# Crossbar DMA transposes, a head started in halves, and matmuls moved up, in a fused attention and feed-forward kernel

The kernel runs on one core of one Trainium2 chip. The metric is device time in microseconds (us) of that core, median over executions; the lower the better. All executions told of here are fast, with a mean granted TensorE clock of 0.995 or more.

## The reference

Eight batches of eight heads, 576 rows of 64 columns. Attention is linear: q is normalized over the columns, k over the rows, both after an exponent, so that kv is a 64 x 64 matrix for each head. Its result, 4608 rows of 512 columns, goes through a gated feed-forward block.

```python
q_s = exp(q);  q_s = q_s / sum(q_s, axis=-1)          # (the reference also subtracts maxima and adds 1e-9)
k_s = exp(k);  k_s = k_s / sum(k_s, axis=2)
kv  = einsum('bhsd,bhse->bhde', k_s, v)
x   = einsum('bhsd,bhde->bhse', q_s, kv)              # then heads side by side: 4608 x 512
g, val = x @ w_gate, x @ w_val                        # 512 x 1536
out = (gelu(g) * val) @ w_out                         # 1536 x 512
```

## The kernel before

One batch follows another. A batch's feed-forward part has twelve steps (a gate and a value group of four matmuls each, then a gelu on ScalarE and a product on DVE) and four output groups of twelve matmuls. All eight PSUM banks are in two pools: six for feed-forward (`ps_big`), two for attention (`ps_att`). Attention of the next batch rides between steps, by a list of callbacks: `at(b, FI, i, ...)` runs after step i of batch b (steps count from 0), and `at(b, NS, i, ...)` after output group i. x needs q transposed, since the contraction runs over its columns. The kernel has two ways to do that: TensorE transposes (batches 0 to 2), and, from batch 3 on, DVE transposes of 32 x 32 blocks followed by 16 small DMAs that put the blocks in place.

```python
    def kv0_mm(hp):                           # batch 0: both heads of a pair in one 128-column matmul
        pool, tag = (ps_att, "att") if hp == 0 else (ps_big, "mm")
        st[("pskv0", hp)] = pool.tile([P, P], f32, name="pskv0", tag=tag)
        for n in range(NC):
            nc.tensor.matmul(
                st[("pskv0", hp)], ek_b[0][:, n, hp * P:(hp + 1) * P],
                v16_b[0][:, n, 2 * hp:2 * hp + 2, 0:D], start=(n == 0), stop=(n == NC - 1))
    # ... cut
    def unit_t32(b, hp):                      # batches 3 to 7: blocks on DVE ...
        # ... cut
        nc.vector.transpose(
            out=et[:, :, hp].rearrange("p c (n i) -> p n c i", i=32),
            in_=eq_b[b % 2][:, :, hp * P:(hp + 1) * P].rearrange("p n (c j) -> p n c j", j=32))

    def moves(b):                             # ... then 16 DMAs
        # ... cut
        for a in range(4):
            for c in range(4):
                nc.sync.dma_start(out=t[32 * c:32 * c + 32, a],
                                  in_=st[(b, "et")][32 * a:32 * a + 32, c])
    # ... cut: the start of batch 0
    cast_v(0, 0, 2, "dve")
    cast_v(0, 2, 4, "act")
    ksum_rec()
    cast_v(0, 4, 6, "act")
    kv0_mm(0); kv0_mm(1); kv0_norm(0); kv0_norm(1)
    cast_v(0, 6, 8, "dve")
    # ... cut: loads, weights
    unit_x(0, 0, "act", True)
    kv0_mm(2)
    unit_x(0, 1, "act", True)
    kv0_norm(2)
    unit_t(0, 1, "dve")
    # ... cut: what rides in batch 1
    at(1, FI, 9, L(unit_t, 2, 0))
    at(1, FI, 10, L(unit_t, 2, 1))
    at(1, FI, 11, L(load_batch, 3), L(exp, "k", 2, 4, 8), L(exp, "q", 3), L(exp, "k", 3), ...)
    at(1, NS, 0, L(unit_trem, 2))
    at(1, NS, 1, L(unit_kv4, 2))
    at(1, NS, 2, L(unit_x4, 2, ("dve", "dve")))
```

The softmax here doesn't subtract the row's maximum and nothing guards it: scores larger than these inputs give would overflow.

## Time and profile before

| | before |
|---|---|
| median of the first three runs | 315.99 us (315.94 to 316.39) |
| profiled run | 316.26 us, span 314.5 us, clock 1.0 |
| TensorE busy | 98% of the span |
| DVE, ScalarE, GpSimd busy | 61%, 44%, 14% |

The runs' times are 1.7 to 1.9 us longer than the spans that the profiler shows. In what follows, times of instructions count from the start of the span. "PE" is TensorE, "ACT" ScalarE, "POOL" GpSimd, and "SPq" the queue from which DMAs are issued. The prediction shows the main lines of before. This is TensorE's list of waits: what it waited for, us in total, how often, and the longest.

```profile
PE pskv L261 <- DVE v L143: 0.4, 1, 0.4
...
PE psx L365 <- DVE kv_sb L267: 0.2, 1, 0.2
```

Both lie in the first 15 us, before feed-forward starts. (The short stalls near 48.84 and 63.21 are not in this list; they are found from starts and counts.) And this is DVE's timeline at the start (start, length, line and operation, output and input):

```profile
14.38 0.73 DVE L143 CAST v<-vt 128x640 f16<-128x640 f32 x1
...
15.61 0.69 DVE L143 COPY eqt<-pst 128x1024 f16<-128x1024 f16 x1 [0.24 <-PE pst L306]
```

DVE casts v's last two heads from 14.38 to 15.11 us. Batch 2's feed-forward begins here on TensorE's timeline:

```profile
85.26 1.03 PE L411 MATMUL psg<-xt,wg_sb 128*128 128x512 f16 x4
```

### The profile page before, as it was taken

The numbers are of one execution on the slowest core, as the hardware profiler recorded it, in microseconds if no ns is written. First come the engines' busy times: TensorE is split into PE (matmuls) and PEld (weight loads), VectorE is DVE, ScalarE is ACT, GpSimd is POOL, SyncE is SP. The second block draws the span as 40 slices with busy tenths as digits, with TensorE's granted clock in tenths as the row PEclk, the third lists the DMA queues.
The fourth block names the chain that finished last, engine by engine and source line by source line (L and its number), as shares of the span: only waits on it lengthen the run. The fifth ranks groups of instructions, "written<-read, shape, count | busy, mean of one in ns | idle before, by whom it ended". The sixth has DMA issues, their size and how long they took to land.

```text
span 314.5 us, 4799 instructions
## 1 busy us (share of the span) xinstructions
PE 307.7 (98%) x1826; PEld 143.7 (46%) x1826; DVE 191.1 (61%) x324; ACT 138.5 (44%) x178; POOL 44.7 (14%) x59
## 2 busy tenths in 40 slices
PE   8899999999999999999999999999999999999995
PEld 3444454444444444444444444444444444444443
DVE  3844386597898479746984599458943434324331
ACT  3753564988433663356334643374330233013300
POOL 2657451331001200030003000300000000000000
PEclk9999999999999999999999999999999999999999
DMA  7999999950178116921492139303021200140002
GB/s 231 372 383 394 401 386 388 395 194 0 69 245 306 53 70 194 349 59 67 127 386 80 72 90 383 115 27 131 1 58 28 115 18 0 35 101 0 3 33 100
DMA packets 42343, 50.78 MB, mean 161 GB/s; under 512 B 3408, under 2 KB 38096, under 8 KB 42320
## 3 DMA queue, kind: packets, MB, share of 16 engines
q1 hardware_dynamic: 40592, 48.84, 45.0%
q10 hardware_dynamic: 1728, 1.64, 1.6%
q8 instruction: 14, 0.23, 0.3%
q14 instruction: 9, 0.07, 0.1%
HBM read 37.75 MB, written 9.44 MB: 150 GB/s over the span
## 4 chain that ended last, share of the span: by engine, by line
PE 90%; DVE 4%; DMA 2%; ACT 2%; issue 1%; ACTq 0%; DVEq 0%
PE psy L489 29%; PE psg L411 28%; PE psv L411 27%; DMA qt<-in_q_dram 2%; PE pskv L284 1%; DVE eq L200 1%; PE psl L510 1%; PE psx L383 1%; DVE rq L191 1%; DVE rq L181 1%; DVE ht L418 1%; PE psx L365 1%; ACT eq L163 1%; PE pst L306 1%; ACT L416 0%
## 5 line engine op out<-in xcount | busy, mean ns | idle before, releaser
L416 ACT ACTIVATE gl<-psg 128x512 f32<-128x512 f32 x108 | 64.0, 599 | 131.0 <-PE psg L411 124.5
L418 DVE SCALAR_TENSOR_TENSOR ht<-psv,gl 128x512 f16<-128x512 f32 x108 | 72.9, 682 | 64.6 <-PE psv L411 64.1
L411 PE MATMUL psg<-xt,wg_sb 128*128 128x512 f16 x384 | 100.5, 379 | 0.1
L411 PE MATMUL psv<-xt,wv_sb 128*128 128x512 f16 x384 | 100.5, 379 | 0.0
L489 PE MATMUL psy<-wo_sb,ht 128*128 128x512 f16 x420 | 94.0, 379 | 0.0
L411 PEld LDWEIGHTS <-wv_sb 128*128 128x128 f16 x432 | 42.3, 98 | 51.2 <-issue 0.8
L411 PEld LDWEIGHTS <-wg_sb 128*128 128x128 f16 x432 | 41.9, 98 | 49.4 <-issue 0.4
L489 PEld LDWEIGHTS <-ht 128*128 128x128 f16 x420 | 40.4, 98 | 47.9 <-issue 0.8
L538 DVE TENSOR_SCALAR yo<-psy 128x512 f32<-128x512 f32 x30 | 20.5, 685 | 29.7 <-PE psy L489 29.7
L139 POOL CAST v<-vt 128x640 f16<-128x640 f32 x26 | 18.8, 763 | 137.1 <-DMA vt<-in_v_dram 98.3
L181 DVE TENSOR_REDUCE rq<-eq 128x10 f32<-128x640 f16 x28 | 22.7, 812 | 6.1 <-ACT eq L163 5.7
L200 DVE TENSOR_TENSOR eq<-eq,rrq 128x640 f16<-128x640 f16 (+1 forms) x29 | 23.7, 817 | 0.3
L163 ACT ACTIVATE ek<-kt 128x1280 f16<-128x1280 f32 (+1 forms) x11 | 19.1, 1746 | 3.4 <-DMA kt<-in_k_dram 3.3
L163 ACT ACTIVATE eq<-qt 128x2560 f16<-128x2560 f32 (+2 forms) x10 | 18.4, 1863 | 2.3 <-DMA qt<-in_q_dram 2.2
L331 DVE STREAM_TRANSPOSE et<-eq 128x640 f16<-128x640 f16 x20 | 16.9, 845 | 0.7
L411 PE MATMUL psg<-xtr,wg_sb 128*128 128x512 f16 x48 | 12.3, 379 | 0.0
L411 PE MATMUL psv<-xtr,wv_sb 128*128 128x512 f16 x48 | 12.3, 379 | 0.0
L143 DVE CAST xt<-psx 128x512 f16<-128x512 f32 x16 | 10.2, 682 | 1.2 <-PE psx L365 1.2
L403 PE MATMUL pswarm<-warm,ident 128*128 128x512 f16 x34 | 9.5, 438 | 1.4 <-POOL ident masks.py:199 1.4
L163 ACT ACT_TABLE_LOAD x8 | 10.3, 1283 | 0.6 <-DMA qt<-in_q_dram 0.5
L141 ACT CAST xt<-psx 128x512 f16<-128x512 f32 x16 | 8.7, 588 | 3.5 <-PE psx L365 3.5
L141 ACT CAST xtr<-psxr 128x128 f16<-128x128 f32 (+1 forms) x6 | 1.7, 283 | 17.8 <-PE psxr L383 17.8
(74 smaller groups left out, 122.6 us busy)
## 6 DMA issues: line engine op xcount, KB each, us to landing
out_dram<-yo SPq DMA_DIRECT2D x14, 512.0 KB, 3.5
kt<-in_k_dram SPq DMA_DIRECT2D x7, 640.0 KB, 7.9
vt<-in_v_dram SPq DMA_DIRECT2D x7, 640.0 KB, 8.4
qt<-in_q_dram SPq DMA_DIRECT2D x7, 640.0 KB, 6.5
qt<-in_q_dram SPq DMA_DIRECT2D x8, 512.0 KB, 6.7
eqt<-et SPq DMA_DIRECT2D x80, 40.0 KB, 1.9
wost<-in_moe_w_out_dram SPq DMA_DIRECT2D x6, 512.0 KB, 7.9
kt<-in_k_dram SPq DMA_DIRECT2D x6, 512.0 KB, 8.1
```

Of the source, the lines that this page charges most:

```text
L139: nc.gpsimd.tensor_copy(out=dst, in_=src)
L141: nc.scalar.copy(out=dst, in_=src)
L143: nc.vector.tensor_copy(out=dst, in_=src)
L163: nc.scalar.activation(out=dst[:, n0:NC, h0 * D:h1 * D].rearrange(o, d=D, **({"t": 2} if b >= QUAD else {})), in_=heads(tiles[(nm, b)], b, ...
L181: nc.vector.reduce_sum(rq, e, axis=mybir.AxisListType.X)
L200: (nc.gpsimd if eng == "pool" else nc.vector).tensor_tensor(out=e, in0=e, in1=rrq.unsqueeze(-1).to_broadcast((P, n, 2, D)), op=ALU.mult)
L331: nc.vector.transpose(out=et[:, :, hp].rearrange("p c (n i) -> p n c i", i=32), in_=eq_b[b % 2][:, :, hp * P:(hp + 1) * P].rearrange("p n ...
L411: nc.tensor.matmul(ps, w[:, ci, fi * P:(fi + 1) * P], xt[:, ci, :], start=(ci == 0), stop=(ci == HP - 1))
L416: nc.scalar.activation(out=gl, in_=psg, func=ACTF.Gelu)
L418: nc.vector.scalar_tensor_tensor(out=ht, in0=psv, scalar=_H_SCALE, in1=gl, op0=ALU.mult, op1=ALU.mult)
L489: nc.tensor.matmul(psy, hts[fi][:, ns * P:(ns + 1) * P], wo_sb[:, fi, :], start=(fi == 0), stop=(fi == NFI - 1))
L538: nc.vector.tensor_scalar(out=yo, in0=psy, scalar1=1.0 / _H_SCALE, scalar2=None, op0=ALU.mult)
```

## The change

Its intent is to take work and stalls off TensorE in the first 85 us: (1) start batch 0's feed-forward earlier, (2) have batch 1's x ready when its feed-forward begins, (3) give one step of batch 1 other PSUM banks, (4) move batch 2's transposes from TensorE to one crossbar DMA, and (5) do the same for batches 3 to 7, where they ran on DVE. (6) is a consequence: batch 3's loads are queued behind batch 2's transpose, and batch 3's sums move into batch 2's first steps. The numbers are those of the prediction.

```diff
@@ (4), (5) the crossbar transpose, one DMA for a batch @@
+    def unit_td(b):
+        t = att.tile([P, NC * C], f16, name="eqt", tag="eqt").rearrange(
+            "p (n h t) -> p n h t", n=NC, h=HP)
+        nc.sync.dma_start_transpose(out=t.rearrange("p n h t -> p (n h) t"),
+                                    in_=eq_b[b % 2].rearrange("p n c -> p (n c)"))
+        st[(b, "eqt4")] = t
@@ (1) kv of batch 0 in halves @@
+            for s in range(2):
+                c0 = hp * P + s * D
+                nc.tensor.matmul(ps[s * D:(s + 1) * D], ek_b[0][:, n, c0:c0 + D],
+                                 v16_b[0][:, n, 2 * hp + s, 0:D], start=(n == 0), stop=(n == NC - 1))
@@ (1) the start (old lines: see above) @@
+    cast_v(0, 0, 1, "dve")
+    cast_v(0, 1, 2, "act")
+    cast_v(0, 2, 3, "dve")
+    cast_v(0, 3, 4, "act")
     cast_v(0, 4, 6, "act")
+    unit_t(0, 1, None, (lambda: kv0_mm(0), lambda: kv0_norm(0), lambda: kv0_mm(1),
+                        lambda: kv0_norm(1), lambda: unit_x_halves(0, 0)))
+    evac_t1 = st["evac_t"]
+    unit_x(0, 1, "act", True)
+    kv0_mm(2)
+    evac_t1("dve")
+    ksum_rec(1)
+    kv0_norm(2)
     cast_v(0, 6, 8, "dve")
@@ (2) end of batch 0, start of batch 1 @@
-    at(0, NS, 16, L(unit_kv, 1, 0), L(cast_v, 1, 4, 8), L(load_batch, 2, ((v, "v"),)))
-    at(0, NS, 6, L(norm, 1, 3))
+    at(0, NS, 16, L(unit_kv, 1, 0), L(cast_v, 1, 4, 8), L(load_batch, 2, ((v, "v"),)),
+       L(norm, 1, 3))
-                cut = 10 if ns == 3 else NFI
+                cut = 9 if ns == 2 else 7 if ns == 3 else NFI
@@ (3) @@
-            hts.append(ffn_fi(xt, fi))
+            hts.append(ffn_fi(xt, fi, b == 1 and fi == 7))     # True: both banks from ps_att
@@ (4), (6) batch 2 @@
-    at(1, FI, 3, L(exp, "q", 2), L(norm, 2, 0))                # and so for steps 4 to 6
+    at(1, FI, 3, L(exp, "q", 2), L(norm, 2, 0, "pool"))
-    at(1, FI, 9, L(unit_t, 2, 0))
-    at(1, FI, 10, L(unit_t, 2, 1))
+    at(1, FI, 9, L(unit_td, 2))
     at(1, FI, 11, L(load_batch, 3), ...)
-    at(1, NS, 0, L(unit_trem, 2))
-    at(1, NS, 1, L(unit_kv4, 2))
-    at(1, NS, 2, L(unit_x4, 2, ("dve", "dve")))
+    at(1, NS, 0, L(unit_kv4, 2))
+    at(1, NS, 1, L(unit_x4, 2, ("dve", "dve")))
@@ (5), (6) batches 3 to 7 @@
-                at(b - 1, NS, hp, L(norm_sum, n, hp))
-                at(b, FI, hp, L(norm_mul, n, hp), L(unit_t32, n, hp))
-            at(b, FI, 4, L(moves, n))
+                at(*((b, FI, hp) if n == 3 else (b - 1, NS, hp)), L(norm_sum, n, hp))
+                at(b, FI, hp, L(norm_mul, n, hp))
+            at(b, FI, 4, L(unit_td, n))
```

Cut are two smaller parts of (1) (sums of k in two tiles, x of the first head pair in two banks) and of (2) (the order of the matmuls that open batch 1), and tile sizes.

More of the change, by code (lines that the diff above doesn't have):

```diff
@@ L103 @@
     QUAD = 2
-    T32 = 3
     def heads(x, b, h0, h1):
@@ L122 @@
     wst = {}
-    ETW = HP * 4 * NC * 32
     def wst_tile(name, n, w):
-        t = wstp.tile([P, ETW], f16, name=name, tag="wst")
-        return t[:, 0:2 * n * w].bitcast(f32).rearrange("p (n w) -> p n w", n=n)
+        return wstp.tile([P, HP * 256], f32, name=name, tag="wst")[:, 0:n * w].rearrange(
+            "p (n w) -> p n w", n=n)
     def load_w_gv(c):
@@ L236, in kv_norm @@
         for j in range(2):
-            kv_sb = att.tile([P, 2, D], f16, name="kv_sb", tag="kv", bufs=12)
+            kv_sb = att.tile([P, 2, D], f16, name="kv_sb", tag="kv", bufs=8)
             nc.vector.scalar_tensor_tensor(
@@ L242, in kv_norm, with ksum_mm, ksum_rec @@
             st[(b, "kv", 2 * g + j)] = kv_sb
-    def ksum_mm(hps):
-        if "pks" not in st:
-            st["pks"] = ps_big.tile([P, HP], f32, name="pks", tag="mm")
-        for hp in hps:
+    def ksum_mm(g):
+        st[("pks", g)] = ps_big.tile([P, 2], f32, name="pks", tag="mm")
+        for j in range(2):
+            hp = 2 * g + j
             for n in range(NC):
-                nc.tensor.matmul(st["pks"][:, hp:hp + 1], ek_b[0][:, n, hp * P:(hp + 1) * P], ones,
-                                 start=(n == 0), stop=(n == NC - 1))
-    def ksum_rec():
-        st["rck0"] = att.tile([P, HP], f32, name="rck0", tag="rck0", bufs=1)
-        nc.vector.reciprocal(out=st["rck0"], in_=st["pks"])
+                nc.tensor.matmul(st[("pks", g)][:, j:j + 1], ek_b[0][:, n, hp * P:(hp + 1) * P],
+                                 ones, start=(n == 0), stop=(n == NC - 1))
+    def ksum_rec(g):
+        st[("rck0", g)] = att.tile([P, 2], f32, name="rck0", tag="rck0")
+        nc.vector.reciprocal(out=st[("rck0", g)], in_=st[("pks", g)])
     def kv0_mm(hp):
-        pool, tag = (ps_att, "att") if hp == 0 else (ps_big, "mm")
-        st[("pskv0", hp)] = pool.tile([P, P], f32, name="pskv0", tag=tag)
+        ps = ps_big.tile([P, D], f32, name="pskv0", tag="mm")
+        st[("pskv0", hp)] = ps
         for n in range(NC):
-            nc.tensor.matmul(
-                st[("pskv0", hp)], ek_b[0][:, n, hp * P:(hp + 1) * P],
-                v16_b[0][:, n, 2 * hp:2 * hp + 2, 0:D], start=(n == 0), stop=(n == NC - 1))
+            for s in range(2):
+                c0 = hp * P + s * D
+                nc.tensor.matmul(ps[s * D:(s + 1) * D], ek_b[0][:, n, c0:c0 + D],
+                                 v16_b[0][:, n, 2 * hp + s, 0:D], start=(n == 0), stop=(n == NC - 1))
     def kv0_norm(hp):
-        kv_sb = att.tile([P, 2, D], f16, name="kv_sb", tag="kv", bufs=12)
+        kv_sb = att.tile([P, 2, D], f16, name="kv_sb", tag="kv", bufs=8)
         nc.vector.scalar_tensor_tensor(
-            out=kv_sb, in0=st[("pskv0", hp)].rearrange("p (h e) -> p h e", e=D),
-            scalar=st["rck0"][:, hp:hp + 1], in1=mask, op0=ALU.mult, op1=ALU.mult)
+            out=kv_sb, in0=st[("pskv0", hp)].unsqueeze(1).to_broadcast((P, 2, D)),
+            scalar=st[("rck0", hp // 2)][:, hp % 2:hp % 2 + 1], in1=mask, op0=ALU.mult, op1=ALU.mult)
         st[(0, "kv", hp)] = kv_sb
@@ L295, in get_eqt, with unit_t @@
         if (b, "eqt") not in st:
-            st[(b, "eqt")] = att.tile([P, HP * 4 * NC * 32], f16, name="eqt", tag="eqt")[
+            st[(b, "eqt")] = att.tile([P, NC * C], f16, name="eqt", tag="eqt")[
                 :, 0:HP * S].rearrange("p (h t) -> p h t", h=HP)
         return st[(b, "eqt")]
-    def unit_t(b, g, eng="dve"):
+    def unit_t(b, g, eng="dve", between=()):
         eqt = get_eqt(b)
         pst = ps_att.tile([P, 2, MAIN], f16, name="pst", tag="att")
+        st["evac_t"] = lambda eng: copy_on(eng, eqt[:, 2 * g:2 * g + 2, 0:MAIN], pst)
         for j in range(2):
             hp = 2 * g + j
+            for f in between if j == 1 else ():
+                f()
             for n in range(NM):
@@ L308, in unit_t @@
                     eq_b[b % 2][:, n + 1, hp * P:(hp + 1) * P], ident)
-        st["evac_t"] = lambda eng: copy_on(eng, eqt[:, 2 * g:2 * g + 2, 0:MAIN], pst)
         if eng:
@@ L324, in unit_trem @@
         nc.vector.tensor_copy(out=st[(b, "eqtr")], in_=pst[:, :, 0:REM] if b == 0 else pst[:, :, 0:P:2])
-    def unit_t32(b, hp):
-        if (b, "et") not in st:
-            st[(b, "et")] = wstp.tile([P, 4, HP, NC * 32], f16, name="et", tag="wst")
-        et = st[(b, "et")]
-        nc.vector.transpose(
-            out=et[:, :, hp].rearrange("p c (n i) -> p n c i", i=32),
-            in_=eq_b[b % 2][:, :, hp * P:(hp + 1) * P].rearrange("p n (c j) -> p n c j", j=32))
-    def moves(b):
-        t = att.tile([P, HP * 4 * NC * 32], f16, name="eqt", tag="eqt").rearrange(
-            "p (a h x) -> p a h x", a=4, h=HP)
-        for a in range(4):
-            for c in range(4):
-                nc.sync.dma_start(out=t[32 * c:32 * c + 32, a],
-                                  in_=st[(b, "et")][32 * a:32 * a + 32, c])
-        t = t.rearrange("p a h (n i) -> p h n a i", i=32)
-        st[(b, "eqt5")] = t
+    def unit_td(b):
[4 more added lines that the diff above has]
+        st[(b, "eqt4")] = t
     def xq(b, hp):
-        if (b, "eqt5") in st:
-            return st[(b, "eqt5")][:, hp, 1:NC]
+        if (b, "eqt4") in st:
+            return st[(b, "eqt4")][:, 1:NC, hp]
         return st[(b, "eqt")][:, hp, 0:MAIN]
     def xqr(b, hp):
-        if (b, "eqt5") in st:
-            return st[(b, "eqt5")][:, hp, 0, :, 0:32:2]
+        if (b, "eqt4") in st:
+            return st[(b, "eqt4")][:, 0, hp, 0:P:2]
         return st[(b, "eqtr")][:, hp, :]
@@ L367, in unit_x, with unit_x_halves @@
         copy_on(eng, xt[:, hp, :], psx)
+    def unit_x_halves(b, hp):
+        for i, eng in enumerate(("act", "dve")):
+            c = slice(i * MAIN // 2, (i + 1) * MAIN // 2)
+            psx = ps_big.tile([P, MAIN // 2], f32, name="psx", tag="mm")
+            nc.tensor.matmul(psx, st[(b, "kv", hp)].rearrange("p h e -> p (h e)"),
+                             xq(b, hp)[:, c], start=True, stop=True)
+            copy_on(eng, get_xt(b)[:, hp, c], psx)
     def unit_xrem(b, eng="act"):
@@ L420, in gate, with ffn_fi, ffn_first @@
         return ht
-    def ffn_fi(xt, fi):
-        psg = ps_big.tile([P, 512], f32, name="psg", tag="mm")
+    def ffn_fi(xt, fi, spare=False):
+        pool, tag = (ps_att, "att") if spare else (ps_big, "mm")
+        psg = pool.tile([P, 512], f32, name="psg", tag=tag)
         mm_gv(psg, wg_sb, xt, fi, range(HP))
-        psv = ps_big.tile([P, 512], f32, name="psv", tag="mm")
+        psv = pool.tile([P, 512], f32, name="psv", tag=tag)
         mm_gv(psv, wv_sb, xt, fi, range(HP))
         return gate(psg, psv)
-    def ffn_first(xt, after, between):
+    def ffn_first(xt, after):
         ps = []
@@ L440, in ffn_first @@
                 mm_gv(psg, wg_sb, xt, fi, range(0, 2))
-                for f in between[fi]:
-                    f()
                 mm_gv(psv, wv_sb, xt, fi, range(0, 2))
@@ L571 @@
     warm_pe(2)
-    ksum_mm((0, 1))
-    warm_pe(2)
-    ksum_mm((2, 3))
-    cast_v(0, 0, 2, "dve")
-    cast_v(0, 2, 4, "act")
-    ksum_rec()
-    cast_v(0, 4, 6, "act")
-    kv0_mm(0)
-    kv0_mm(1)
-    kv0_norm(0)
-    kv0_norm(1)
+    ksum_mm(0)
+    ksum_rec(0)
+    ksum_mm(1)
+    cast_v(0, 0, 1, "dve")
+    cast_v(0, 1, 2, "act")
+    cast_v(0, 2, 3, "dve")
+    cast_v(0, 3, 4, "act")
+    cast_v(0, 4, 6, "act")
+    unit_t(0, 1, None, (lambda: kv0_mm(0), lambda: kv0_norm(0), lambda: kv0_mm(1),
[6 more added lines that the diff above has]
+    kv0_norm(2)
     cast_v(0, 6, 8, "dve")
@@ L590 @@
     cast_w("wv", 0, "pool")
-    unit_x(0, 0, "act", True)
-    kv0_mm(2)
-    unit_x(0, 1, "act", True)
-    kv0_norm(2)
-    unit_t(0, 1, "dve")
     preload(ACTF.Gelu)
@@ L616 @@
     at(0, NS, 5, L(unit_t, 1, 0))
-    at(0, NS, 16, L(unit_kv, 1, 0), L(cast_v, 1, 4, 8), L(load_batch, 2, ((v, "v"),)))
-    at(0, NS, 6, L(norm, 1, 3))
+    at(0, NS, 16, L(unit_kv, 1, 0), L(cast_v, 1, 4, 8), L(load_batch, 2, ((v, "v"),)),
+       L(norm, 1, 3))
     at(0, NS, 17, L(unit_x, 1, 0, "act", True), L(unit_x, 1, 1, "act", True))
     at(0, NS, 7, L(preload, ACTF.Gelu))
-    first1 = ([[L(unit_kv, 1, 1), L(unit_t, 1, 1)], [], [L(unit_x, 1, 3, "dve")]],
-              [[], [], [L(unit_x, 1, 2, "act")]])
+    first1 = [[L(unit_t, 1, 1), L(unit_kv, 1, 1)], [L(unit_x, 1, 2, "act")],
+              [L(unit_x, 1, 3, "dve")]]
     def x_upper0():
@@ L630 @@
     at(1, FI, 2, L(unit_trem, 1))
-    at(1, FI, 3, L(exp, "q", 2), L(norm, 2, 0))
-    at(1, FI, 4, L(norm, 2, 1), L(unit_xrem, 1))
-    at(1, FI, 5, L(norm, 2, 2))
-    at(1, FI, 6, L(norm, 2, 3))
+    at(1, FI, 3, L(exp, "q", 2), L(norm, 2, 0, "pool"))
+    at(1, FI, 4, L(norm, 2, 1, "pool"), L(unit_xrem, 1))
+    at(1, FI, 5, L(norm, 2, 2, "pool"))
+    at(1, FI, 6, L(norm, 2, 3, "pool"))
     at(1, FI, 7, L(exp, "k", 2, 0, 4), L(cast_v, 2, 0, H))
-    at(1, FI, 9, L(unit_t, 2, 0))
-    at(1, FI, 10, L(unit_t, 2, 1))
+    at(1, FI, 9, L(unit_td, 2))
     at(1, FI, 11, L(load_batch, 3), L(exp, "k", 2, 4, 8), L(exp, "q", 3), L(exp, "k", 3), L(exp_rem0), L(cast_v, 3, 0, H))
-    at(1, NS, 0, L(unit_trem, 2))
-    at(1, NS, 1, L(unit_kv4, 2))
-    at(1, NS, 2, L(unit_x4, 2, ("dve", "dve")))
+    at(1, NS, 0, L(unit_kv4, 2))
+    at(1, NS, 1, L(unit_x4, 2, ("dve", "dve")))
     at(2, FI, 7, L(norm_rem0))
@@ L651 @@
             for hp in range(HP):
-                at(b - 1, NS, hp, L(norm_sum, n, hp))
-                at(b, FI, hp, L(norm_mul, n, hp), L(unit_t32, n, hp))
-            at(b, FI, 4, L(moves, n))
-            if n == T32:
+                at(*((b, FI, hp) if n == 3 else (b - 1, NS, hp)), L(norm_sum, n, hp))
+                at(b, FI, hp, L(norm_mul, n, hp))
+            at(b, FI, 4, L(unit_td, n))
+            if n == 3:
                 at(b, FI, 5, L(unit_kv4, n))
@@ L670 @@
         if b < 2:
-            hts = ffn_first0(xt, (x_upper0, L(unit_x, 0, 3, "act"))) if b == 0 else ffn_first(xt, *first1)
+            hts = ffn_first0(xt, (x_upper0, L(unit_x, 0, 3, "act"))) if b == 0 else ffn_first(xt, first1)
             fi0 = len(hts)
```

## The prediction

> **What bounds the kernel now.** I read the busy shares first, then the costliest groups, then TensorE's timeline in the places where the change works, then the DMA queue's timeline.
>
> The busy shares, the costliest groups and the summary of the chain that ended last:
>
> ```profile
> PE 307.7 (98%) x1826; PEld 143.7 (46%) x1826; DVE 191.1 (61%) x324; ACT 138.5 (44%) x178; POOL 44.7 (14%) x59
> PE 90%; DVE 4%; DMA 2%; ACT 2%; issue 1%; ACTq 0%; DVEq 0%
> ...
> L489 PE MATMUL psy<-wo_sb,ht 128*128 128x512 f16 x420 | 94.0, 379 | 0.0
> L331 DVE STREAM_TRANSPOSE et<-eq 128x640 f16<-128x640 f16 x20 | 16.9, 845 | 0.7
> ```
>
> TensorE is the bound: 98% busy, 90% of the last chain, at full granted clock throughout. 379 ns is the latency of one pipelined matmul; starts within a run of them lie 215.8 ns apart (the timeline's four-matmul groups start every 0.86 us). The feed-forward part is 1296 such matmuls (counting the split last rows as twelve): 1296 x 0.2158 = 279.7 us, which the change leaves alone. About 35 us of the 314.5 us span is open: the start, attention's own matmuls, stalls. DVE's 191 us matter only where TensorE waits for it.
>
> TensorE's timeline, start and length of a group in us; a group's pitch is its count x 0.216 (512 columns) or x 0.056 (128 columns), so what a start lacks against the last start plus pitch is a stall:
>
> ```profile
> 12.51 0.40 PE L250 MATMUL pks<-ones,ek 128*128 128x1 f16 x10
> 13.36 0.72 PE L261 MATMUL pskv<-v,ek 128*128 128x128 f16 x10 [0.45 <-DVE v L143]
> 14.24 0.39 PE L365 MATMUL psx<-eqt,kv_sb 128*128 128x512 f16 x1 [0.17 <-DVE kv_sb L267]
> ...
> 15.41 0.38 PE L411 MATMUL psg<-xt,wg_sb 128*128 128x512 f16 x1
> 16.55 0.38 PE L365 MATMUL psx<-eqt,kv_sb 128*128 128x512 f16 x1
> ...
> 48.23 0.59 PE L489 MATMUL psy<-wo_sb,ht 128*128 128x512 f16 x2
> 48.84 0.38 PE L411 MATMUL psg<-xt,wg_sb 128*128 128x512 f16 x1
> ...
> 62.10 1.03 PE L411 MATMUL psv<-xt,wv_sb 128*128 128x512 f16 x4
> 63.21 1.02 PE L411 MATMUL psg<-xt,wg_sb 128*128 128x512 f16 x4
> ...
> 68.39 0.61 PE L306 MATMUL pst<-ident,eq 128*128 128x128 f16 x8
> 68.89 1.02 PE L411 MATMUL psg<-xt,wg_sb 128*128 128x512 f16 x4
> ...
> 70.61 0.92 PE L306 MATMUL pst<-ident,eq 128*128 128x128 f16 x8
> 71.36 1.03 PE L411 MATMUL psg<-xt,wg_sb 128*128 128x512 f16 x4
> ```
>
> The start waits for v's cast and kv's norm. Batch 1's first gate matmul is 0.18 us late (48.84 against 48.66), the gate matmul at 63.21 is 0.25 us late (no free PSUM pair while ScalarE loads tables and takes exponents), and batch 2's transposes occupy 0.50 + 0.75 us. From batch 3 on the timeline has no stall, only some 0.09 us at each side of the small tiled matmuls.
>
> **What the Trainium skill says.** "TensorE: Matmul & The Clock Gate", Back-to-back issue gap, gives N/2.4 + 2.5 ns; the trace agrees (215.8 ns for 512 columns). "TensorEngine Tiling (Array Packing)", Key Properties, says that a change of tiling mode drains TensorE; the trace agrees, at about 0.09 us each way around the 64-column kv matmuls. For the crossbar transposes two pages disagree, and nothing in this trace shows one: "DMA: Bandwidth & Descriptors", Latency and other measured facts, has 261 GB/s for a DMA transpose; "VectorE: DVE Perf Modes", The three transpose paths, has 1309 ns for one 128x128 block. Each DMA here takes 20 blocks, 655,360 bytes: an estimate of 2.5 us plus about 2 us fixed (a small copy lands in 1.9 us here) from the first, 26 us from the second if blocks went one after another.
>
> **The change part by part.**
>
> (1) The start. The first kv is now multiplied in 64-column halves from v cast one head at a time, and the first x goes into two PSUM banks, evacuated by ScalarE and DVE together. v lands at 12.6 us (ScalarE and DVE both start its casts there), so this does not move. A 640-element cast takes 0.67 us, so one head some 0.37; after the 0.17 us reciprocal, now ahead of it, it ends near 13.15. Ten 64-column matmuls at the 19 ns of batch 2's kv, plus about 0.17 us to the result, let the kv norm start at 13.6, against 13.83. But what stands behind it on DVE has grown: two norms (0.30 each), the half evacuation (0.35, waiting for its matmul until 14.4), the second transpose's evacuation (0.60, formerly at 15.61, now first), a reciprocal (0.17), the third norm (0.33), and only then the cast of v's last two heads (0.66), formerly at 14.38: it ends near 16.6. The fourth kv waits for that cast. The first gate matmul comes earlier, 15.05 against 15.41, but after four of them TensorE waits about 0.6 us, and the next x matmul starts at 16.88 against 16.55. **+0.3 us**, not a gain.
>
> (2) The end of batch 0. kv, norm and two x of batch 1 move three to five output matmuls earlier, so ScalarE casts x beside five remaining matmuls (1.08 us). That removes 0.18 at 48.84, 0.06 two matmuls on, and 0.19 before 53.13, where the last x was cast too late: **-0.43 us**.
>
> (3) Feed-forward step 7 of batch 1 takes its two banks from attention's pool, whose tiles (transposed remainder, x remainder) are evacuated by 57.7 and 63.4: **-0.25 us**.
>
> (4) Batch 2's 20 TensorE transposes go: 0.50 + 0.75 + 0.22 (four more at 75.68) = **-1.47 us**, if the crossbar DMA lands in time. It waits for four norm multiplies, now on GpSimd at 1.26 us each (one at 44.74). DVE's sums come between its gate products: sums end near 62.4, 64.9, 66.5 and 68.1, so the last multiply ends near 69.4. The x matmuls come after output group 1. With the gains above, feed-forward ends near 71.5, group 0 at 74.1, kv adds 0.95, group 1 ends at 77.6. The DMA has **about 8 us**.
>
> (5) From batch 3 on the 20 DVE transposes (16.9 us) and 80 small DMAs become five crossbar DMAs. DVE was off the path there and the x matmuls keep their sizes: **0 us**. Each is issued after step 3's multiply, some 10 us into a batch, and is needed 28 us in: 18 us.
>
> (6) A wait that the diff hides: the DMA queue works in order, and batch 2's transpose is queued ahead of batch 3's loads.
>
> ```profile
> 52.69 1.34 SPq L117 DMA_DIRECT2D qt<-in_q_dram  x2
> 54.07 3.52 SPq L117 DMA_DIRECT2D kt<-in_k_dram  x2
> 60.92 1.28 SPq L117 DMA_DIRECT2D vt<-in_v_dram  x2
> ```
>
> q and k of batch 3, issued at 52.7 and 54.1 now, can't be issued before 69.4. At 6 to 9 us to landing, plus what the transpose holds the queue, q arrives at 77 to 80 and k at 80 to 83; ScalarE then needs 2.3 us for k, 0.6 for a rest and 1.3 for the table before the first gelu of batch 2, at 84 to 88. That batch starts at 83.6 and has three pairs of banks, but DVE also takes batch 3's sums in its first four steps (0.60 + 0.81 + 0.22 + 0.82 = 2.45 us per step of 1.73). I allow **+0.5 us**, 0 to 1.
>
> Sum: 0.3 - 0.43 - 0.25 - 1.47 + 0.5 = -1.35. The runs' median of 315.99 is 1.5 us above the span and moves with it; I round up the gain a little, as a tuned order may hide some of (6), to 314.4.
>
> **Rivals.** A, *slow crossbar*: if a transpose takes over 8 us, batch 2's x waits for the excess and batch 3's loads and exponents shift by as much again. At 12 us that costs 4 us there and perhaps 4 in batch 2: about 321. At the second page's 26 us it costs some 18 us, plus 8 in each of five batches: over 370. For it: the pages disagree and the trace has no such DMA. Against it: the new order moves kv and x of batch 2 one group *earlier*, which nobody would do with a late transpose. B, *the start pays*: if the split kv and x let feed-forward begin 0.36 us earlier and the last cast of v fits in DVE's gaps, (1) is -0.3 and the time about 313.6. C, *all hidden*: if feed-forward after batch 1 is held back by ScalarE's exponents instead, (3) and half of (4) come back as a wait for a gelu: about 315.5.
>
> **Range and chances.** The parts give 312.9 (B, and no stall from (6)) to 316 (C with a 1 us stall); a transpose of 10 us takes it to 317. Range 313.0 to 317.0. Faster by over 2% means under 309.7, which all open stalls together don't reach: 1%. Slower by over 2%, above 322.3, needs rival A: 6%. Within 2%: 93%.
>
> **What would show it.** Right: no TensorE transposes between 68 and 76 us, no late gate matmul near 48.8 and 63; a crossbar DMA issued near 69 and landed before 77; q of batch 3 loaded after it; a TensorE wait of about 0.6 us near 16 us for the last cast of v; DVE busy near 175 us; nothing new on TensorE from batch 3 on. Wrong: x matmuls waiting for a transpose DMA (A), gate matmuls of batch 2 waiting for gelu or DVE by over 1 us, or a start without the wait near 16 us (B).

## The result, and the profile after

| | before | after |
|---|---|---|
| median, same rounds | 316.15 us (315.94 to 316.39), 4 runs | 314.5 us (314.45 to 314.55), 4 runs |
| span of the profiled run | 314.5 us | 312.6 us |

The ratio is 0.9948, with a 95% interval of 0.993 to 0.9965: 0.5% faster, within the 2% that count as the same. Ratios here are the mean time of one kernel's fast runs over that of the other's of the same rounds, so not quite the ratio of the medians that are quoted.

The page's busy shares and the summary of its chain that ended last, after:

```profile
PE 306.3 (98%) x1825; PEld 142.7 (46%) x1825; DVE 172.3 (55%) x300; ACT 138.4 (44%) x179; POOL 48.2 (15%) x63
...
PE 94%; DVE 3%; DMA 2%; ACT 0%; issue 0%; DVEq 0%; ACTq 0%
```

DVE loses 18.8 us of work, and the span a tenth of that, 1.9 us. In the chain TensorE now has 94% instead of 90%: the bound is the same engine, with less in between. TensorE's timeline at the start, after:

```profile
14.98 0.39 PE L409 MATMUL psg<-xt,wg_sb 128*128 128x512 f16 x1
...
15.66 0.38 PE L409 MATMUL psv<-xt,wv_sb 128*128 128x512 f16 x1
16.63 0.35 PE L260 MATMUL pskv<-v,ek 128*64 128x64 f16 x10 [0.60 <-DVE v L140]
16.91 0.39 PE L354 MATMUL psx<-eqt,kv_sb 128*128 128x512 f16 x1
```

The first gate matmul comes 0.43 us earlier (14.98 against 15.41), but after four of them TensorE waits 0.60 us for the cast of v, and the third x matmul is 0.36 us *later* (16.91 against 16.55). DVE's timeline has the reason: what the change put ahead of that cast.

```profile
14.71 0.68 DVE L140 COPY eqt<-pst 128x1024 f16<-128x1024 f16 x1
...
15.84 0.74 DVE L140 CAST v<-vt 128x640 f16<-128x640 f32 x1
```

The cast begins 1.46 us later than before (15.84 against 14.38). TensorE's timeline from the end of batch 0 to batch 2, after:

```profile
47.95 1.24 PE L486 MATMUL psy<-wo_sb,ht 128*128 128x512 f16 x5
49.03 0.38 PE L409 MATMUL psg<-xt,wg_sb 128*128 128x512 f16 x1
...
62.91 1.03 PE L409 MATMUL psg<-xt,wg_sb 128*128 128x512 f16 x4
...
71.55 2.75 PE L486 MATMUL psy<-wo_sb,ht 128*128 128x512 f16 x12
...
77.68 0.26 PE L381 MATMUL psxr<-eqt,kv 64*64 64x64 f16 x8
...
83.49 1.03 PE L409 MATMUL psg<-xt,wg_sb 128*128 128x512 f16 x4
...
88.67 1.03 PE L409 MATMUL psg<-xt,wg_sb 128*128 128x512 f16 x4
```

Five output matmuls take 5 x 0.2158 = 1.08 us, and 47.95 + 1.08 = 49.03: the 0.18 us of before are gone. 62.91 is exactly one group of four after the matmuls at 62.05: no wait for banks. Between there and 71.55 there is no transpose. Batch 2 begins at 83.49, 1.77 us earlier than before (85.26), and from there to the fourth step, 88.67 = 83.49 + 24 x 0.2158, TensorE never waits. The DMA queue's own timeline (start, time that the issue held the queue, DMA), and two lines from the list of instructions that read or write the transposed tile (durations in ns):

```profile
69.41 3.20 SPq L330 DMA_TRANSPOSE eqt<-eq  x1
72.67 1.29 SPq L116 DMA_DIRECT2D qt<-in_q_dram  x2
74.01 1.31 SPq L116 DMA_DIRECT2D kt<-in_k_dram  x2
```

```profile
L330 SPq DMA_TRANSPOSE eqt<-eq x6: 3092/4484/7284, 69.4 to 223.7; - x6
...
DMA to landing us min/median/max: 4.9/6.4/9.4
```

Batch 2's transpose was issued at 69.41 and landed 5.0 us later, at 74.4: 3.3 us before x needs it (77.68). Batch 3's loads of q and k follow it 20 us later than before. ScalarE's timeline shows how that goes on:

```profile
78.95 2.34 ACT L160 ACTIVATE eq<-qt 128x2560 f16<-128x2560 f32 x1 [4.89 <-DMA qt<-in_q_dram]
82.92 2.34 ACT L160 ACTIVATE ek<-kt 128x2560 f16<-128x2560 f32 x1 [1.63 <-DMA kt<-in_k_dram]
...
87.09 1.57 ACT L414 ACTIVATE gl<-psg 128x512 f32<-128x512 f32 x3
```

ScalarE waits for both loads, and batch 2's first gelu comes at 87.09, 3.6 us after its gate matmuls began. The first of the three ends near 87.7 (a single gelu takes 0.60), and the fourth step, which needs its bank, starts at 88.67: about 1 us to spare.

### The profile page after: what moved, and what is told of

The parts are those of the page before. It is cut to its first block, busy times and chain, and to the rows that moved or that the text cites. A ratio compares the mean times of both kernels' runs of the same rounds, so it can differ in the third digit from the quotient of the medians.

```text
span 312.6 us, 4697 instructions
## 1 busy us (share of the span) xinstructions
PE 306.3 (98%) x1825; PEld 142.7 (46%) x1825; DVE 172.3 (55%) x300; ACT 138.4 (44%) x179; POOL 48.2 (15%) x63
## 4 chain that ended last, share of the span: by engine, by line
PE 94%; DVE 3%; DMA 2%; ACT 0%; issue 0%; DVEq 0%; ACTq 0%
PE psg L409 30%; PE psv L409 30%; PE psy L486 29%; DMA qt<-in_q_dram 2%; PE pskv L282 1%; PE psl L507 1%; PE psx L381 1%; DVE rq L188 1%; PE psx L354 0%; DVE eq L197 0%; PE pskv L224 0%; DVE eqt L140 0%; PE psxr L381 0%; DVE v L140 0%; ACT eq L160 0%; PE pst L307 0%
## 5 line engine op out<-in xcount | busy, mean ns | idle before, releaser
L416 DVE SCALAR_TENSOR_TENSOR ht<-psv,gl 128x512 f16<-128x512 f32 x108 | 73.8, 689 | 79.7 <-PE psv L409 74.1
L136 POOL CAST v<-vt 128x640 f16<-128x640 f32 x26 | 17.7, 724 | 115.6 <-DMA vt<-in_v_dram 115.6
L197 DVE TENSOR_TENSOR eq<-eq,rrq 128x640 f16<-128x640 f16 (+1 forms) x25 | 20.2, 808 | 0.3
L197 POOL TENSOR_TENSOR eq<-eq,rrq 128x640 f16<-128x640 f16 (+1 forms) x7 | 9.3, 1322 | 24.9 <-DVE rrq L180 17.3
L140 DVE CAST xt<-psx 128x512 f16<-128x512 f32 (+1 forms) x17 | 10.7, 668 | 1.4 <-PE psx L354 1.3
L138 ACT CAST xt<-psx 128x512 f16<-128x512 f32 (+1 forms) x16 | 8.6, 575 | 3.1 <-PE psx L354 2.9
```

What stands on the lines that cost most here:

```text
L136: nc.gpsimd.tensor_copy(out=dst, in_=src)
L138: nc.scalar.copy(out=dst, in_=src)
L140: nc.vector.tensor_copy(out=dst, in_=src)
L197: (nc.gpsimd if eng == "pool" else nc.vector).tensor_tensor(out=e, in0=e, in1=rrq.unsqueeze(-1).to_broadcast((P, n, 2, D)), op=ALU.mult)
L416: nc.vector.scalar_tensor_tensor(out=ht, in0=psv, scalar=_H_SCALE, in1=gl, op0=ALU.mult, op1=ALU.mult)
```

## The experiments

Each is an edit of the changed kernel, and each gave a correct result. Kernels of one group shared a chip and its runs of the kernel before: 316.29 us (9 runs) for the first, 316.16 (11) for the second, 316.15 (12) for the third. Since the chip of the second and third group was not that of the first, differences across groups are checked by the ratios. "More" and "less" are against 314.43 us, the median of the first of these runs.

### First group: the start, and batch 2's transposes

**The changed kernel again**, unedited.

> The changed kernel as it is, for comparison on this chip. Both theories: 314.5 us (314.3 to 314.7), span 312.6 us, a TensorE wait of 0.60 us for the cast of v's last two heads at 16.0 us, no wait between 17 us and the end other than the 0.09 us at changes of tiling.

314.43 us (314.39 to 314.77, 5 runs), ratio 0.9945 (0.9932 to 0.9957). As before, and the base that the others are compared with.

**The last cast of v on GpSimd.**

```diff
-    cast_v(0, 6, 8, "dve")
+    cast_v(0, 6, 8, "pool")
```

> One word changed: the last two heads of batch 0's v are cast by GpSimd, which is free from 12.9 us until the first weights come, and not by DVE at the end of its queue. Theory (the split start is held back only by that cast, behind DVE's longer queue): the 0.60 us wait goes, the x matmul of head pair 2 starts near 16.15 us in place of 16.91, and the time falls by 0.75 us against the changed kernel, to 313.75 us. Rival (the start is bound by the weights that GpSimd casts): the 0.7 us that GpSimd spends on v come back as a wait for gate or value weights, time 314.3 to 314.6 us.

313.77 us (313.64 to 314.18), ratio 0.9924 (0.9911 to 0.9936); 0.66 us less than the changed kernel. The 0.60 us wait is gone, so it was the place of that cast in DVE's queue that cost it.

**The start of before.** The old start sequence, `kv0_mm` and `ksum_mm` are put back; all else stays changed.

> The changed kernel with the start of before: kv of batch 0 on full columns, v cast in pairs, x in one bank, second transpose after the first x. Theory (the new start costs 0.36 us, because its cast of v's last heads comes too late): x of head pair 2 near 16.55 us in place of 16.91, time 314.15 us. Rival (the split kv and x pay, as feed-forward begins 0.4 us earlier with them): 314.8 to 314.9 us.

314.18 us (314.12 to 314.3), ratio 0.9936 (0.9922 to 0.9949): 0.25 us *less* than the changed kernel. The new start costs what was predicted (0.3). Rival B, that it gains 0.3, falls.

**Batch 2's transposes back on TensorE**, its norm back on DVE, kv and x one output group later.

```diff
-    at(1, FI, 9, L(unit_td, 2))
+    at(1, FI, 9, L(unit_t, 2, 0))
+    at(1, FI, 10, L(unit_t, 2, 1))
```

> Batch 2 back to TensorE's 20 transposes with the norm on DVE and x one output group later, the rest as in the changed kernel. Theory (the transposes were 1.47 us on the bound engine, two of the groups waiting for the norm): time up by 1.3 to 1.5 us, to 315.8 to 316.0 us. Rival (without them another engine held that stage, and half of it was hidden): up by 0.5 to 0.8 us.

317.31 us (316.71 to 317.84), ratio 1.003 (1.0017 to 1.0043): 2.9 us more than the changed kernel, where 1.3 to 1.5 were expected. The expectation missed. TensorE's timeline of this run has a line that was not in it:

```profile
71.20 0.61 PE L307 MATMUL pst<-ident,eq 128*128 128x128 f16 x8 [0.84 <-DVE ht L416]
```

The matmuls before it ended at 70.19 by count, so the second transpose waits 1.0 us, for DVE's product of step 7. The new guess: part (3) lets step 7 take attention's two banks, and the transposes need the same two. The third group tests it.

### Second group: the other parts, one at a time

**Batches 3 to 7 back on DVE blocks** and small DMAs. (Cut: the two functions and the larger staging tile, which come back with them.)

```diff
-                at(b, FI, hp, L(norm_mul, n, hp))
-            at(b, FI, 4, L(unit_td, n))
+                at(b, FI, hp, L(norm_mul, n, hp), L(unit_t32, n, hp))
+            at(b, FI, 4, L(moves, n))
```

> Batches 3 to 7 back to DVE's 20 block transposes and 80 small DMAs, batch 2 on the crossbar. Theory (nothing on TensorE waited for them): DVE busy up by about 17 us, to 189 us, and the time the same within 0.15 us, 314.35 to 314.65 us. Rival (the freed DVE is worth something from batch 3 on, where its steps take longer than TensorE's): up by 0.3 to 1 us, with waits for the gate product in batch 2, whose norm sums now stand in the same steps.

317.77 us (317.5 to 320.15, 6 runs; the two above 319 have a clock of 0.995 and lift the ratio), ratio 1.0072 (1.0045 to 1.0099): 3.3 us more by the medians. A clear miss, and against the prediction's "0 us" for (5). TensorE's timeline of this run, in batch 2:

```profile
98.80 1.02 PE L434 MATMUL psv<-xt,wv_sb 128*128 128x512 f16 x4 [1.41 <-DVE ht L441]
...
102.53 1.02 PE L434 MATMUL psv<-xt,wv_sb 128*128 128x512 f16 x4 [1.85 <-DVE ht L441]
```

By count, these start 1.57 and 2.01 us late, 3.6 us together. In batch 2's first four steps DVE has a product (0.65), a sum (0.81), a reciprocal (0.22), a multiply (0.83) and now a block transpose (0.84): 3.35 us for a step of 1.73. Two things make this batch different from the later ones: the sums were moved here, and the gelus start late (6). Whether the block transposes do harm without these two is tested in the third group.

**Step 7 of batch 1 from the common pool**, so (3) undone.

```diff
-            hts.append(ffn_fi(xt, fi, b == 1 and fi == 7))
+            hts.append(ffn_fi(xt, fi))
```

> Feed-forward step 7 of batch 1 takes its banks from the common pool again. Theory: its first gate matmul waits about 0.25 to 0.3 us for the gelu of step 4, as in the kernel before, and the time rises by as much, to 314.75 to 314.8 us. Rival (the wait only moves into slack that step 11 has towards ScalarE's gelus): same time.

314.63 us (314.6 to 314.77), ratio 0.9951 (0.9939 to 0.9964): 0.2 us more. The two intervals overlap, so the time alone does not show it; the trace does, where the step starts 0.25 us late by count. (3) is worth what was predicted (0.25).

**The end of batch 0 as before**, so (2) undone (the diff of the change, backwards).

> The end of batch 0 and the first steps of batch 1 as before: kv after the third output group, norm of the last head pair later, x two matmuls before the end. Theory: three waits of 0.18, 0.06 and 0.19 us near 49 and 53 us come back, time 314.9 us. Rival (they were caused by the later start of before): same time, 314.5 us.

314.9 us (314.84 to 316.38, 6 runs; the highest, with a clock of 0.995, lifts the ratio), ratio 0.9969 (0.9954 to 0.9983): 0.47 us more by the medians, and the three waits are back in the trace, 0.18, 0.06 and 0.19 us. (2) is worth 0.43, as predicted.

**q and k of batch 3 loaded ahead of the transpose.**

```diff
-    at(1, FI, 9, L(unit_td, 2))
-    at(1, FI, 11, L(load_batch, 3), ...)
+    at(1, FI, 9, L(load_batch, 3, ((q, "q"), (k, "k"))), L(unit_td, 2))
+    at(1, FI, 11, L(load_batch, 3, ((v, "v"),)), ...)
```

> q and k of batch 3 are queued ahead of batch 2's crossbar transpose, v after it. Theory (the loads' delay of 17 us is inside ScalarE's slack, as the trace of the changed kernel shows no TensorE wait in batch 2): the exponents of batch 3 start near 74 us in place of 79, the first gelu of batch 2 is over 3 us earlier, and the time is the same within 0.1 us. Rival (the prediction's term of 0.5 us, hidden in the spacing of matmuls): 0.3 to 0.5 us faster.

314.41 us (314.37 to 314.52), ratio 0.9945 (0.9933 to 0.9957): no change. ScalarE's first gelu of batch 2 now comes at 84.47 instead of 87.09, and the time is the same. So the late loads, the half of (6) that this edit undoes, cost nothing in the changed kernel, where 0.5 us were allowed for (6).

### Third group: the two misses, and a combination

**DVE blocks, but with q and k of batch 3 early and its sums back in batch 1's output groups.** On top of the edit for DVE blocks:

```diff
-                at(*((b, FI, hp) if n == 3 else (b - 1, NS, hp)), L(norm_sum, n, hp))
+                at(b - 1, NS, hp, L(norm_sum, n, hp))
```

and the edit of the run before.

> The run with DVE's block transposes for batches 3 to 7 lost 3.3 us, which the prediction had put at 0. Its trace shows two waits of TensorE, 1.57 and 2.01 us, for gate products in batch 2. Here the block transposes stay, and what stands in their way goes: q and k of batch 3 are loaded ahead of batch 2's crossbar transpose, and batch 3's norm sums go back to the output groups of batch 1. Theory (the block transposes hurt only because sum, multiply and transpose of one head pair make 3.3 us of DVE per step of 1.73 us, after a late first gelu): both waits go, 314.3 to 314.6 us. Rival (block transposes beside a crossbar transpose cost something by themselves): at least 315.5 us.

314.35 us (314.26 to 314.38), ratio 0.9942 (0.9928 to 0.9956). All 20 block transposes and 80 DMAs are in it (DVE is busy 187.1 us again), and it is as fast as the changed kernel. The block transposes cost time only on top of late gelus and moved sums. Which of these two matters more was not tried.

**Batch 2's transposes on TensorE, and step 7 from the common pool** (both edits shown above).

> The run with batch 2 on TensorE lost 2.8 us, twice the expected 1.47; its trace shows a wait of 1.0 us at the second group of transposes, behind DVE's gate products. Here feed-forward step 7 has its banks from the common pool again as well. Theory (the second group waits for attention's two banks, which step 7 holds until its gate product): that wait shrinks to the 0.30 us of the kernel before, step 7 waits 0.25 us, and the time is 316.1 us (315.9 to 316.4). Rival (the wait comes from the norm alone, which DVE multiplies later than GpSimd did): the 1.0 us stays, 317.3 us or more.

316.2 us (315.83 to 316.48), ratio 1.0 (0.9987 to 1.0013). Giving up (3) as well makes it about 1 us *faster* than with (3) (ratio 1.0 against 1.003). On TensorE's timeline of this run the second transpose follows its matmuls without a wait (69.47 + 4 x 0.2158 = 70.33), and step 7 waits the 0.25 us of before:

```profile
69.47 1.03 PE L409 MATMUL psv<-xt,wv_sb 128*128 128x512 f16 x4
70.34 0.61 PE L307 MATMUL pst<-ident,eq 128*128 128x128 f16 x8
```

The conflict over banks is shown. Against 314.43 this undoes (3) and (4) together: 1.77 us by the medians, where the prediction has 0.25 + 1.47 = 1.72. The profiled execution, the fastest of the four (315.83 us), is only 1.40 us over; item 4 below says what is missing in it.

**Batch 2's transpose twice**, the second over the same tiles, so that it waits for the first.

```diff
-    at(1, FI, 9, L(unit_td, 2))
+    at(1, FI, 9, L(unit_td, 2), L(unit_td_again, 2))      # the same DMA once more
```

> Batch 2's crossbar transpose is done twice into the same tile, the second after the first has landed. Right result, a longer wait. Theory (rival A of the prediction, at a known length): the second lands near 79.4 us, x of batch 2 waits about 1.7 us; the loads of batch 3 are issued 5 us later, gelu of batch 2 starts near 92 us, and DVE's sums behind it cost another 3 to 4 us: 319 to 320.5 us in all. Rival (loads and gelu have enough slack, only the landing counts): 316.1 to 316.3 us.

318.85 us (318.48 to 318.96), ratio 1.0083 (1.007 to 1.0096): 4.4 us more than the changed kernel, a little under what was expected. The DMA queue's timeline, then TensorE's, of this run:

```profile
74.57 3.09 SPq L336 DMA_TRANSPOSE eqt<-eq  x1
```

```profile
79.49 0.25 PE L386 MATMUL psxr<-eqt,kv 64*64 64x64 f16 x8 [1.55 <-DMA eqt<-eq]
...
92.58 1.02 PE L414 MATMUL psg<-xt,wg_sb 128*128 128x512 f16 x4 [1.93 <-ACT gl L419]
...
103.33 1.02 PE L414 MATMUL psv<-xt,wv_sb 128*128 128x512 f16 x4 [0.24 <-DVE ht L421]
```

Against the changed kernel x starts 1.6 us later after the matmuls before it; by count the fourth step of batch 2 starts 2.1 us late, and a later one loses 0.4 us to DVE. This is what rival A said of a slow crossbar: once the margin of 3.3 us is used up, x waits for the excess, and batch 3's loads, which stand behind in the queue, make batch 2 wait for gelus as well. Only the second part was put too high in the expectation (3 to 4 us instead of 2.5).

**A combination that should beat both**: the last cast of v on GpSimd, and the third and fourth kv of batch 0 on full columns again.

```diff
+        if hp >= 2:                        # one 128-column matmul, as in the kernel before
+            st[("pskv0", hp)] = ps_big.tile([P, P], f32, name="pskv0", tag="mm")
+            # ... cut
-    cast_v(0, 6, 8, "dve")
+    cast_v(0, 6, 8, "pool")
```

> The changed kernel with v's last two heads cast by GpSimd and with the third and fourth kv of batch 0 on full columns again, as each change of tiling costs 0.09 us where TensorE has no wait to hide it. Theory: 0.1 us less for each of the two against the run with the cast on GpSimd alone, 313.5 to 313.65 us. Rival (weights or output weights, cast by GpSimd, take over at the front): 313.75 us or more, with a wait near 40 us.

314.17 us (313.79 to 314.49), ratio 0.9935 (0.992 to 0.9949). A miss: no faster than the cast on GpSimd alone, which is what the rival said; but the wait is near 20 us and not near 40. TensorE's timeline of this run shows a wait for weights in step 2, and GpSimd's shows why:

```profile
20.72 1.04 PE L417 MATMUL psv<-xt,wv_sb 128*128 128x512 f16 x4 [0.57 <-POOL wv_sb L136]
```

```profile
19.62 1.04 POOL L136 CAST wv_sb<-wvst 128x1024 f16<-128x1024 f32 x1 [1.69 <-DMA wvst<-in_moe_w_val_dram]
```

In the run with only the cast moved, the same cast came sooner, on GpSimd's timeline there:

```profile
18.33 1.04 POOL L136 CAST wv_sb<-wvst 128x1024 f16<-128x1024 f32 x1 [0.37 <-DMA wvst<-in_moe_w_val_dram]
```

It was used at 20.16 there, 0.8 us after it ended, so feed-forward cannot start much earlier before the weights set the pace. Why the weights landed 1.3 us later in this run is open: the load was issued at 12.5 us in both, and the runs of this kernel are spread over 0.7 us. The lowest median is that of the cast on GpSimd alone, 313.77 us, but the intervals of the two runs overlap.

## Why the prediction was right

The predicted 314.4 us met 314.5, and the class was right. The sum behind it was right term by term, but for one, and part of the close hit is luck (see below the list).

1. **The start, +0.3: right.** First gate matmul at 15.05 (measured 14.98), the cast's end at 16.6 (16.58), a wait of 0.6 (0.60), x at 16.88 (16.91). The old start put back gave 0.25 us, the cast on another engine took the wait away.
2. **End of batch 0, -0.43: right.** The three waits are gone; the step that follows the remainder's transposes starts at 55.89 against 55.94, although the start had lost 0.36, which makes 0.41; and undoing it cost 0.47 us.
3. **Banks for step 7, -0.25: right**; undoing it cost 0.2 us. What was not seen: these are the banks that TensorE transposes in batch 1 would have needed. (3) is only good together with (4): without (4) it costs about 1 us by the medians, 0.7 in the two profiled executions.
4. **Batch 2's transposes, -1.47: right for the two profiled executions.** The crossbar DMA was issued at 69.41 (predicted 69.4) and x at 77.68 (77.6), so it had the 8 us, and took 5.0. Of the two figures, the rate was near: the 655,360 bytes moved in about 3 us at some 215 GB/s, against an estimate of 2.5 us plus 2 fixed. Twenty blocks one after another at 1309 ns, 26 us, did not happen. Rival A falls for this kernel, and the doubled transpose shows that it was a real danger: 5 us more would have been 4.4 us lost. But 0.30 of the 1.47 is a wait inside the second group of transposes (70.61, 0.92 us long), for a norm multiply on DVE that took 1.23 us where the three before it took 0.82 or 0.83. With the transposes back and (3) undone it took 0.86, there was no such wait, and the trace has only 1.16 us for (4). How often the wait comes is not known.
5. **Batches 3 to 7, 0: right for the time, with a gap in the reason.** "DVE was off the path there" holds only if the sums and the loads stay where they were. In batch 2 with (6), DVE would have been the bound: with the block transposes kept, 3.3 us are lost. So the crossbar for batches 3 to 7 gains nothing on its own (314.35 without it), but it is what lets (6) be free. Its margin was also smaller than the 18 us predicted: batch 3's transpose was issued at 97.98, 14.5 us into the batch and not 10, and landed 4.9 us later, 10 us before x (112.93).
6. **Batch 3's loads behind the transpose, +0.5: the one term that was mis-sized; it measured 0.** Its mechanism is in the trace: q's exponent at 78.95 (77 to 80 predicted for q), k's at 82.92 (80 to 83), first gelu at 87.09 (84 to 88). But three pairs of banks take TensorE from 83.49 to the fourth step at 88.67, and the first bank was free about 1 us earlier. The allowance was made from the middle of a range, not from this comparison, which the prediction had the numbers for: 83.6 + 5.2 = 88.8, against a first gelu that ends at 88.6 at the latest. The other half of the term, DVE's sums, made no step late either, though with little left: 0.84 us more in each of those four steps (DVE blocks) made 3.6 us of waits. The value groups that wait there, and in the run with the transpose twice, start right after the product of four steps earlier; in the changed kernel the closest such product ends near 98.4, for a group at 99.02, which leaves 0.6 us.

With 0 in place of 0.5, the sum is 0.3 - 0.43 - 0.25 - 1.47 = -1.85 us. With the measured shifts in their places it is 0.36 - 0.41 - 0.25 - 1.47 = -1.77, exactly the shift of batch 2's first matmul (85.26 to 83.49). TensorE's last output group moved by 1.76 (308.06 to 306.30), so nothing was gained or lost on TensorE in between; the rest of the 1.9 us of the span lies after it. The medians moved by 1.65. From 315.99 the sum of -1.35 gives 314.64; the prediction took another 0.24 off, since the order "may hide some of (6)". All of (6) was hidden, so this allowance, which rests on no number, made up half of the mis-sized term: luck as much as judgement. Two sums of the rivals are off, which changed nothing: A's "about 321" is 314.4 + 8 = 322.4, and the 312.9 of B without (6) is 314.4 - 0.6 - 0.5 = 313.3. Rival C, that ScalarE's exponents give the gain back in batch 2, falls too: there is no wait for a gelu.

Not settled: in the run with batch 2 on TensorE, the profiled execution was 2.0 us over the changed kernel's span, of which 1.0 is the wait for banks; the median of its runs was 2.9 us over. The trace cannot speak for the other 0.9. In the run with both edits, too, the profiled execution was the fastest, 0.37 us below its median.

## What to carry to other kernels

A large saving on an engine that is off the path (19 us of DVE here) is worth only the waits that it takes from the bound engine, so price a change by the starts of that engine's instructions, stage by stage. Parts of a change can be worth something only together: a borrowed bank, a later load and a freed engine each looked neutral or good alone, and undoing one and not its partner cost 2.9 us in one case and 3.3 in another. When work is pulled forward on an in-order queue, look at what was last in it, since that is what the next wait will be for; here moving one cast to an idle engine gave a further 0.66 us.

## What the Trainium skill lacked or had wrong

- "VectorE: DVE Perf Modes", The three transpose paths: its 1309 ns for one 128x128 block through the crossbar can't be multiplied by the number of blocks. 20 blocks in one DMA landed 5.0 us after issue, with the data moving for some 3 us.
- "DMA: Bandwidth & Descriptors", Latency and other measured facts: 261 GB/s for a DMA transpose with a non-contiguous middle dimension, and some 350 to 400 for a contiguous one; the profile shows some 215 GB/s for this one between SBUF tiles, alone on the DMA engines.
- "TensorE: Matmul & The Clock Gate", Back-to-back issue gap, which the prediction cites: the page calls N/2.4 + 2.5 ns the gap of an isolated matmul, and puts a 512-column matmul in a stream at some 131 ns. Here streams with a weight load for each matmul run at 215.8 ns, so it is the formula that holds in them.
- Neither that table of transpose paths nor those measured facts of DMA say how long a crossbar DMA holds the issuing queue. Here it was 3.1 to 7.3 us (median 4.5), and loads behind it were issued later by as much (batch 3's q at 72.67, after 69.41 + 3.20). The six of the changed kernel landed 4.9 to 9.4 us after issue (median 6.4): 4.9 or 5.0 us in three, 7.8 to 9.4 in the three whose issue came within 5 us of the loads of a batch.
